# Half-height transposes in two row tiles, and a filter spectrum stored with both runs of a partition together

## The chip, the cores and the metric

The kernel runs on one core of a Trainium2 chip. The metric is the device time of one execution in microseconds, as the median of several runs. A profiled execution is one further run; its span goes from its first to its last instruction.

## What is computed

A gated recurrence over 6272 steps, followed by a gated long convolution, for 4 batches of 256 channels:

```python
sig = 1.0 / (1.0 + np.exp(-f_logit))
f = lower_bound + (1.0 - lower_bound) * sig
i = 1.0 - f
for t in range(S):                       # S = 6272
    h = f[:, t] * h + i[:, t] * x[:, t]
    y[:, t] = h
...
proj = y @ w_proj                        # 256 -> 3 * 256: x1, x2, x3
X2 = np.fft.rfft(x2, n=S, axis=1)
H = np.fft.rfft(filter_fft, n=S, axis=0)
x2_conv = np.fft.irfft(X2 * H, n=S, axis=1)
out = (x1 * x2_conv * x3) @ w_out
```

The inputs and the output are float32, x and f_logit are 4 x 6272 x 256.

## The kernel before

The Fourier transforms are written as matrix products. 6272 is 49 x 128, so a transform is done as one over 128 points and one over 49, each with a small table of cosines and sines as one operand on TensorE. Channels are worked in 16 units of 8 pairs.

**Opening.** `prepare` builds the tables, loads the filter (L576), rotates it with matmuls (L587), transforms it (`first`, L612, and `second`, L630), and writes the spectrum of each unit to device memory (`hst`, L638), because it doesn't fit beside the rest. TensorE is kept running with warm-up matmuls (`warm`, L557); four of the 32 warm-up groups (L555) are made of eight half-height transposes each. At the same time `hgrn(0)` computes the recurrence of the first batch.

**Recurrence.** `hgrn(b)` goes through 13 chunks of 512 time steps (the last has 128). A chunk of x and f_logit is loaded with time along the partitions, four steps to each (L302, into XT and FL, three buffers each). ScalarE takes the sigmoid in place (`sig`, L304), GpSimd multiplies it onto x (`u`, L306). For each half of the channels (kh) TensorE turns both so that channels lie along the partitions and time along the row: `sT` for the sigmoid and `uT` for the product, each of four transposes of 128 x 128 into one PSUM bank (L313). A transpose takes one of the four columns of a partition and so writes every fourth element of the bank. `f` makes the gate from the bank of sT (L327 on ScalarE, L329 on VectorE), and `scan` runs the recurrence on VectorE over the bank of uT (L335) into HA, which holds the whole sequence of a batch, with a wrapped copy of its front part (`wrap`).

**Spectrum.** `phase_p` projects the columns (P, L670) and evacuates them into X2 (`x2`). For each unit, F1 (L683) and its evacuation `A` do the first step, F2 (L728) the second, two `prod` on VectorE (L741) multiply by the spectrum in Hu, I2 (L751) starts the inverse and `Th` evacuates. `mini`, `zm` and `slot` do a few special frequencies. Hu has three buffers; `H` (L718) fills one per unit and batch. In device memory a unit's spectrum is a matrix of 98 + 64 rows of 2 KB: rows 0 to 97 are the spectrum, and rows 98 to 161 repeat its first 64. Partition p needs rows p and p + 49, and `twice` (L265) describes that read.

**Gates and output.** `gate` computes x1 and x3 (x13, L362), evacuates them (`xs`) and multiplies them on GpSimd (`z`, L378). `phase_o` ends the inverse (I1, L784), multiplies on VectorE (`y`, L790), projects (L802), evacuates (`o`) and stores (L812).

F2, mini, I1, FF2 (`second`) and `last` work with matmuls of 64 rows, two at a time in the upper and the lower half of the array, which write to two neighbouring PSUM banks. All other TensorE work uses the full height, or 98 rows of it.

**What sets the order.** Each step is recorded by `Plan.op` with its kind, its cost on each engine that may do it, what it reads and writes, and how many PSUM banks it takes (`take`). Nothing is scheduled when the kernel is built: `ORDER` (L117) is a table made beforehand, three letters for each step, which give the step, the engine and the first PSUM bank. `Plan.emit` goes through it once. So each engine has its own fixed sequence, DMAs are all issued by SyncE (SP) in the table's order, and a step starts when it is at the head of its engine and its semaphores allow it.

In time, the work of a batch stands so that P is followed by a stage of units (F1, F2, prod, I2, and x13 of the gates) and one of output (I1, y, proj). The recurrence of the next batch is laid into the unit and output stages of the one before; there is none after the last transposes at 392.8 us.

Of the kernel before, what the change touches and what calls it, by code (L numbers as in the profile page):

```python
# [10 lines left out]
F32R = mybir.dt.float32r  # L11
# [10 lines left out]
S = 6272  # L22
D = 256
# [35 lines left out]
class Plan:  # L59

    ROWS = ("F2", "mini", "I1", "FF2", "last")
# [56 lines left out]
    "BLgAAYA8gAOYABIAsQBBgACIBGgA0RBagBVgAbSBQgBkgAfUA7YAPIAtVADgAdWBfgA9YAwQERgA+RBCAApTAqUBABBpgAoVBHABDWARIAuQ"  # L118
    "BugBMYBEGAgTBFGA6UA/BBITBzgBNVBJDA2QBKDB4gAjXBRYBPFAkRAQAAlSESgBWYA5QEfgBSTAnXBTLBbYBXRBOFEggAmQBUDBZJAYYBcV"
    "BgAAUIA3XBYJEtgAvQASABlIBhTBeFAeREugBjDA4XBqIBiDBmQETAAcSAFgBoIBvYAzXBnIAxUBrSBdNBwQB0YAWIBtCAiXBsKB5AArUATI"  # L120
    "ByAAEYB6VB1SB8NBxAEUYB7NAhXB3KB2CEVUCBVEXMEhAB/QCKSEWXCLCEaUEiYEYPCCFCISE7gCAACTVCJCEcMCEQCNSCFICDYEbXAVYCUF"
    "CMYEjUEvAE8gEdPEkWCcQEwYEoVElMCdAEpXFJgCOCEmOCaQCHgExUFKgCbACRSCQgEzMEqFEyWCSCClQE0OE9ACVYCWUCeYCfSCmAErPE+Y"
    "E2WCXEE3QCgKE/RE4GCZgCjUFXgFBBCsWFYgE5IAZYCkECGgFASFLAFETFCKC1UFlgCtGCnYCoQFMYCPgAHAFGLCuWCpIFFSCvGFNTC2EC3W"
    "FHKAaYFPDFOQFZAFSRFQIFTUFxgC4GFbVCwYCigAIADHSFmgC5YFUJFaYAJAFygC6WFdFFVMCrgCxQCYgC7GAyVChgDIKC+UB9YCyIDJWC/E"
    "DASDKGFcUFnADBKFgVFeMDDQDCYF9gALADLYAXYFzACqgDMWDEIDQSFiFFoYFhUDRCDSQFjMF+gDbSDTAFpVAMADZQAKAFrNF0YFqUDaAFtV"
    "FsMDNGFuQGJgF1RGKgDVWDcKF3BDUYF2UFvNDdYDWGFRYDkSFwIFWYF5RF/ADeVGVgF4MF7BF6XC0gDlCGAYDtQGWgDfFDiSDuIGBUDjKDrV"
    "GLAGDMD0QEeYGCSDsFF8PDmYGFTGMYDnUGhgGEKGHDGGWD1AGNXGigGIOD2SGPHCzgDvYGOQGXAGRRD3KD9WGtgGQIGTBDwSGYYC9gFkAC8g"
    "GSRD+GGZQE6AGUJGugD/WGbADGgDFgE1YGjAGaQEAOD4YDXgGdRGcIEBYGeWGkYAGgGfBGlXDOgDoEGgOD5QDYgFIAEGUDPgDxKGnHMwgFfY"
    "GmWEHEEsYGpXGvAGoOEIUGrHGwYGqSEJEGxTGyXGsKA1WD6AEKYFDYG1UEPVANAGzLECQEQFG0PEZYELSEnYJsXG3EG5gMvgEMCB+YG2VJtW"
    "DpgG4NM9gJxUJvGG8SEOgEDAHGVG9KEEgD8gHAQHHFDqgJzMENgJySNLgHBIJuHHKTJ0CJwYDygMxAHCVHLLHOQMyYHDFEFgHESDzgHPAM+g"  # L130
    "G6UHFCJ1YJ2XHSQJ4HHMSHTIM/AHQWG7EHIQHROHNCG+UHJAHegJ3WG/MMzXHlgJ5GJ7SD7gNNAJ6YJ8TM1PDggHUQDhgJ9KJ+DNMgHWUHVI"
    "KAWJ/YHXEKBXHYSKDHHfQNAYHZCHmUHiIKFXKCGHaSKHHHhIKGWKEYM0RKIGM4XHoMHbCHzgKKQKJYKLWHsgKMAHcSM2JKPUKNGKQQM6HKOY"
    "KUWHdKKSAM5RHpMKRENBXHgYKWGH8SKTYNDHNCQM7JIEgH6UH9CNZgHnYKVWKZXH7EKXONGRNEIHjSKYYKbHNIBHtUM8AH0WHwMKaQHkCKeR"
    "KcAHvMHqSKgBKdYKfVHrCH3OH+QILgKjUM3YNagH/AIASH1YKlMHuYKkXNOYKhFH2OHxQIBCIFUHyIISgKmHICSNHWNngNbAIDKIgQKiYKoX"
    "IHMIhAKpSKnYKtTKrCNJOH4QKqHKuUH5AKsYIIMKySKzXKwEIMQKvDIGYK1PIZgIiUK0CKxYNogIOIK3WIjENPTINYNQXIPIK2YNRDK4SK5G"
    "IJUNSPK6CIqgNcYITQIKEIkSIWINpANUWNVXN1gNWGIVINdUIUYN2gNqYIlCIQVNXPIxgIaQNfEImSIRFIcIK8UInCIbYIXVK7YIdIK9XIYF"
    "LBQIoSK/HIrVI4gIpKLDALCRItNK+ENeXN3ALGSLAYLHTNgPIeULEBIsYLICLFYJGQIuNLJDNiXIfENjSODgIzYNkPNrTNTYJHAI/gJIULKY"
    "NlKIyWNtDIvQJJEN4YI1OLLTLMSLNDI0OI5UIwANsXLOCNYYI7MLQTJQgJKQLPYOEgLSDLRWI8MJLANwSI6YLVUOPgNyCI2QNuPJXgJASI3A"
    "LTOLWVJMQJDKLUYLYFLaXJNANxWJCKN5VNvYOQgLXEJOQLbTN7FLZYJPIJegN6ULcHNzOLfSNhAN+VJBYNmYLhCI9QObgN8MOAFJRWLdDLgS"
    "I+AJUOLeYLkVJETOFAJTOJSYJYQJZYLmFOGYN/XJFDJbIJlgOHVLiCOcgJVTOJFJaIJfRJWDLjYLlWJiJORAJcTLpVLnGJhJLqQLoYOISLsA"  # L140
    "OLWLrFOBPJmQJgYJdDJnYOSYSJVJoIJjTONGSLFOMXJpIJkDSKWOogOTQLtYOngSMGSOVOKKOdAJqTOUROOPOeYOVAOXWOYSJrDOzgOfQOWJ"
    "O0gOZGLuTSQFLzWLvLOhASPROgVSRBL0OOjQOpALwTO/gOaKL4WOqYLxDOkRL5OOlAOrSPAgL1TO1ALygOmJNFYL6WL2DO2YOiNL9QL7GL3g"
    "MCTL+IOsVN0AOvWNKYOCAMDLOwXOtCN9YPLgL/QL8gOxGOuNPMgMESMAAOyPO3UMBgMHVO5EMMQMINMFCO4XO7UPBAMNIMJSVMgPNAMGgPCY"
    "O9EO8VO6PPDWMKCMOQO+NMLgMRSMPAPOYMWUMSKPFGMbQPEXVOAMXMPHWMTSPJGVagPGPMQgMYUQJgMUCMcIPIWMZEPPXPQSPTTPKOMdQVog"
    "PRHVNgPUUPSKVQVMVgPVDMgWVbgPWMVSFP7gMlSMhOMagPrUMeAMmKPjWPsEPlQPkGPnSPZUPoCPfWPaMVqAPbSPmAPgOPdUPcCPhQPeEPXW"
    "PiAPpSPYOVcAPvUPtQPwMPqCMiWPuAMqSMnUMjGMrKSNYMkgPxQMoEQCgPzSPyIVPYP3WP0CP1UP4OSTQP2EP8RSVASSYQDWP+JP5TSUVSYQ"
    "P6LSWFSZRSaAP/JP9YQXTSXYSbBSdVQYDQZQQGOQQgSeSQEYMfgScYQaAQATQFOSiXSfFQLYSjQSgCQBLQhgQKVSlAShYQHRSkHQMNSnQSmY"
    "QIBSoTQNNQRUSqDQSYQiRSpAQTMQogQOWSrYVpgSsTQUMQPGStQVdYSxUQkJQVWQvgSzESuDQbUQWGQlJSyTVRRQcEQdWSvIVVSS0DVTJSwY"
    "VWUQeGV2gS2VQ2gS3QVXCS1YV3gQpWS4FQfRS7TQgJS5AVeVS9DQrOQqYQ/QS6YVgFVfSRAAVjTVYMS8VQjYWEgTAWS+FVhKQ9QTCGS/YTBU"
    "VlDMsVQsOQ+ATFSTDETGTMtNTHKQwQV4AMugTEYTILRHgQmVTKXVrYQnFQzIQtSTMHRBUQyIQuCQ3WRCETLRTJYQ6OROgRDSVkQRECTPUQ4Y"  # L150
    "Q5OQxYVsVTNBQ0STREVmITOYRVgRIWVuFWFgTQRQ1CRKOQ7UTSBRjSRLOQ8ETTYRFQRkCRWURGIRcgRPWWGATUSRJYRSORQYV5YRlQTWCTVT"
# [722 lines left out]
```

## Time and profile before

| | us |
|---|---|
| median of 3 runs | 485.76 (485.37 to 486.49) |
| profiled execution | 484.15 |
| its span | 482.3 |
| transposes (L313), 784, busy | 121.5 |
| prod (L741), 128, busy | 147.1 |
| scan (L335), 104, busy | 122.8 |
| f on ScalarE (L327), one of 512 | 0.700 |
| first P group of the four batches starts at | 79.4, 182.2, 289.2, 394.0 |

"Busy" of an engine is the time in which at least one of its instructions ran; instructions overlap with the next one, so that the mean duration of one, times their number, is more than they occupy. What they occupy when the engine is full is the distance from one start to the next. The memory traffic is 116.39 MB, 64 reads of the spectrum with 392 KB each, and 16 writes each of 196 and of 128 KB. The granted clock of TensorE is 0.997 on average.

### The profile page before, as it was taken

What the parts mean: (1) busy time and instruction counts of PE and PEld (TensorE: products, weight loads), DVE (VectorE), ACT (ScalarE), POOL (GpSimd) and SP (SyncE); (2) the same over time, 40 slices, a digit from 0 to 9 for tenths busy, and PEclk for the clock granted to TensorE, in tenths of its full rate; (3) what the DMA queues carried; (4) which work ended last, traced back from release to release, by engine and by line L of the source; (5) the groups of instructions that cost most, each with busy time, mean ns of one, the idle gap of its engine ahead of it and who ended that gap; (6) DMA issues with size and microseconds to landing.
All of it is one profiled execution on the core that took longest, in us unless ns stands there. A gap on an engine that the chain in (4) does not pass through costs nothing.

```text
span 482.3 us, 13258 instructions
## 1 busy us (share of the span) xinstructions
PE 467.0 (97%) x5273; PEld 374.9 (78%) x5273; DVE 425.5 (88%) x456; ACT 416.5 (86%) x609; POOL 298.4 (62%) x307
## 2 busy tenths in 40 slices
PE   8999999999999999999999999999999999999995
PEld 6887877877778999776778889667788998676694
DVE  8879997699999995899999998999999975999983
ACT  5979989999999888989989785999989978999664
POOL 6769775679778620787789533677698332755700
PEclk9999999999999999999999999999999999999998
DMA  8989989847685989476668989364778864345266
GB/s 331 377 277 297 330 283 279 283 153 238 197 296 176 305 293 310 130 250 211 207 211 270 349 280 331 114 195 157 265 264 307 319 228 154 102 132 153 66 262 274
DMA packets 41725, 116.39 MB, mean 241 GB/s; under 512 B 4384, under 2 KB 6304, under 8 KB 41664
## 3 DMA queue, kind: packets, MB, share of 16 engines
q1 hardware_dynamic: 41664, 115.56, 71.5%
q8 instruction: 41, 0.67, 0.6%
q14 instruction: 20, 0.16, 0.1%
HBM read 84.54 MB, written 31.00 MB: 240 GB/s over the span
## 4 chain that ended last, share of the span: by engine, by line
PE 70%; DMA 9%; DVE 7%; ACT 6%; issue 3%; POOL 2%; SPq 0%; POOLq 0%; DVEq 0%; ACTq 0%
PE PS L313 14%; PE PS L362 14%; PE PS L751 8%; PE PS L670 7%; PE PS L802 7%; PE PS L728 6%; PE PS L683 5%; DMA X<-in_moe_filter_fft_dram 4%; DMA out_dram<-osb 4%; PE PS L612 3%; PE PS L784 3%; DVE PP L741 2%; DVE HA L335 2%; ACT osb L275 2%; PE PS L630 2%
## 5 line engine op out<-in xcount | busy, mean ns | idle before, releaser
L378 POOL TENSOR_TENSOR zt<-x1s,x3s 128x490 f16<-128x490 f32 (+1 forms) x104 | 125.8, 1217 | 85.0 <-DVE ys L790 27.5
L741 DVE TENSOR_TENSOR PP<-PS,Hu 98x1008 f16<-98x1008 f32 x128 | 147.1, 1198 | 4.4 <-PE PS L728 1.4
L306 POOL TENSOR_TENSOR XT<-XT,FL 128x1024 f32<-128x1024 f32 (+1 forms) x52 | 116.9, 2251 | 47.0 <-ACT FL L304 28.9
L335 DVE TENSOR_TENSOR_SCAN HA<-fTs,HA,PS 128x512 f16<-128x512 f32 (+1 forms) x96 | 113.0, 1203 | 4.4 <-PE PS L313 1.6
L362 PE MATMUL PS<-HA,W 128*128 128x490 f16 (+1 forms) x416 | 107.2, 368 | 0.0
L327 ACT ACTIVATE fTs<-PS,nomc 128x512 f32<-128x512 f32 (+1 forms) x90 | 60.5, 674 | 7.5 <-PE PS L313 3.9
L275 ACT ACTIVATE osb<-PS 128x1024 f32<-128x1024 f32 (+1 forms) x51 | 49.9, 992 | 17.8 <-PE PS L802 12.0
L790 DVE TENSOR_TENSOR ys<-PS,zt 128x1024 fp32r<-128x1024 f32 (+1 forms) x52 | 59.0, 1153 | 6.9 <-PE PS L784 2.2
L313 PE MATMUL PS<-iden,XT 128*128 128x128 f32 x392 | 61.2, 276 | 0.9 <-ACT fTs L327 0.4
L273 ACT CAST HA<-PS 128x1024 f16<-128x1024 f32 x57 | 57.9, 1027 | 2.8 <-PE PS L683 2.1
L313 PE MATMUL PS<-iden,FL 128*128 128x128 f32 x392 | 60.3, 274 | 0.0
L751 PEld LDWEIGHTS <-PP 98*128 98x128 f16 x1024 | 50.0, 98 | 11.2 <-issue 3.5
L273 ACT COPY x3s<-PS 128x490 f32<-128x490 f32 (+1 forms) x93 | 53.5, 577 | 4.6 <-PE PS L362 2.9
L275 ACT ACTIVATE x1s<-PS 128x490 f32<-128x490 f32 (+1 forms) x93 | 53.9, 591 | 3.7 <-PE PS L362 2.0
L802 PE MATMUL PS<-Wo,ys 128*128 128x256 f32 x392 | 56.4, 291 | 0.6 <-DVE ys L790 0.2
L304 ACT ACTIVATE FL<-FL 128x1024 f32<-128x1024 f32 (+1 forms) x52 | 53.1, 1024 | 1.7 <-DMA FL<-in_f_logit_dram 1.7
L362 PEld LDWEIGHTS <-W 128*128 128x128 f16 x416 | 34.6, 98 | 23.3 <-issue 6.4
L751 PE MATMUL PS<-VA,PP 98*128 98x98 f16 x512 | 52.0, 207 | 0.7 <-POOL PP L733 0.3
L313 PEld LDWEIGHTS PS<-iden,XT 128*128 128x128 f32 x392 | 44.7, 140 | 9.5 <-issue 3.0
L273 ACT CAST Th<-PS 128x784 f16<-128x784 f32 x58 | 47.8, 826 | 4.9 <-PE PS L751 4.0
L802 PEld LDWEIGHTS PS<-Wo,ys 128*128 128x128 f32 x392 | 49.2, 188 | 3.5 <-DVE ys L790 1.2
L751 PE MATMUL PS<-VB,PP 98*128 98x98 f16 x512 | 51.7, 207 | 0.0
(114 smaller groups left out, 695.9 us busy)
## 6 DMA issues: line engine op xcount, KB each, us to landing
Hu<-H SPq DMA_DIRECT2D x64, 392.0 KB
FL<-in_f_logit_dram SPq DMA_DIRECT2D x48, 512.0 KB
XT<-in_x_dram SPq DMA_DIRECT2D x48, 512.0 KB
out_dram<-osb SPq DMA_DIRECT2D x48, 512.0 KB
X<-in_moe_filter_fft_dram SPq DMA_DIRECT2D x9, 512.0 KB
H<-Hu SPq DMA_DIRECT2D x16, 196.0 KB
H<-Hu SPq DMA_DIRECT2D x16, 128.0 KB
Hu<-in_moe_filter_fft_dram SPq DMA_DIRECT2D x2, 512.0 KB
```

Of the source, the lines that this page charges most:

```text
L273: nc.scalar.copy(dst, src)
L275: nc.scalar.activation(dst, src, AF.Copy, scale=scale)
L306: op("u", {"POOL": 0.1 + 0.553 * nb}, lambda e, xt=xt, ft=ft: nc.gpsimd.tensor_tensor(xt, xt, ft, op=AOP.mult), r=[("ft", k)], w=[("xt", k)])
L313: nc.tensor.transpose(PS[:, p, j:128 * nb:nb], src[:, j, cols], iden[:])
L327: nc.scalar.activation(fT, PS[:, p, 0:n], AF.Identity, scale=by, bias=1.0)
L335: nc.vector.tensor_tensor_scan(h, fT, PS[:, p, 0:n], init, op0=AOP.mult, op1=AOP.add),
L362: nc.tensor.matmul(PS[:, p, 0:n], W13[:, kh, js], HA[:, HB[kh] + t0:HB[kh] + t0 + n], start=(kh == 0), stop=(kh == 1))
L378: nc.gpsimd.tensor_tensor(late["zt"][:, jb, :, m0:m0 + nm], xs(0), xs(1), op=AOP.mult),
L741: nc.vector.tensor_tensor(PP[:TB, k, o, :, :, 1:64], px.unsqueeze(1).broadcast_to([TB, 2, UE, 63]), hh[:, :, :, 1:64], op=AOP.mult)
L751: nc.tensor.matmul(PS[:, ib + o, pr * TB:(pr + 1) * TB], PP[:TB, k, o, n, 2 * pr:2 * pr + 2, :], v[:TB], start=(n == 0), stop=(n == 1))
L790: nc.vector.tensor_tensor(late["ys"][:, yk, :, 0:rn * 128], PS[:, cb:cb + 2, 0:rn * 128], late["zt"][:].rearrange("p k r m -> p k (r m)") ...
L802: nc.tensor.matmul(po[:, i, :], late["ys"][:, yk, kh, i * 128:(i + 1) * 128], Wo[:, kh, :], start=(kh == 0), stop=(kh == 1))
```

## The change

There are three parts.

1. `sT` and `uT` become one step `su`. Each transpose of 128 rows becomes two of 64 rows, in the upper and the lower row tile, and 16 of these make a `su` (four in the last chunk). The upper half writes into the first of two neighbouring banks, the lower half into the second. The sigmoid lies in the outer quarters of the two banks (elements 0 to 255 and 768 to 1023), the product in the middle (256 to 767). So `f` reads two runs, and `scan` one run that crosses from one bank into the other. `su` reads both the sigmoid and the product, and takes two banks.
2. The spectrum of a unit is kept in memory as 98 x 2 rows of 2 KB, so that the two rows that a partition needs lie side by side and are read as one run of 4 KB. It is written with three transfers (98, 49 and 49 rows) in place of two (98 and 64).
3. `ORDER` is a new table, with 2350 steps in place of 2438. The four warm-up groups of half-height transposes become warm-up matmuls like the others.

```diff
-    ROWS = ("F2", "mini", "I1", "FF2", "last")
+    ROWS = ("su", "F2", "mini", "I1", "FF2", "last")
...
-    H = [dram.tile([TB + 64, 2 * UE * 64], F16, name=f"H{u}") for u in range(NU)]
+    H = [dram.tile([TB, 2, 2 * UE * 64], F16, name=f"H{u}") for u in range(NU)]
...
+    def bank(pb):
+        return PS[:, pb:pb + 2].rearrange("p a t -> p (a t)")
+    def halves(pb, hn):
+        a = PS[:, pb, 0:hn]
+        return bass.AP(tensor=a.tensor, offset=a.offset,
+                       ap=[a.ap[0], [768, 2], a.ap[1]])
...
-                def turn(e, p, src, cols=cols, nb=nb):
-                    for j in range(nb):
-                        nc.tensor.transpose(PS[:, p, j:128 * nb:nb], src[:, j, cols], iden[:])
-                sT = op("sT", {"PE": 0.109 * nb}, lambda e, p, f=turn, s=ft: f(e, p, s),
-                        r=[("ft", k), "iden"], w=["qT"], take=1)
-                uT = op("uT", {"PE": 0.109 * nb}, lambda e, p, f=turn, s=xt: f(e, p, s),
-                        r=[("xt", k), "iden"], w=["qT"], take=1)
+                hn = 64 * nb
+                def turn(e, pb, ft=ft, xt=xt, cols=cols, nb=nb, hn=hn):
+                    for src, at in ((ft, (0, 768)), (xt, (512 - hn, 512))):
+                        for j in range(nb):
+                            for p in range(2):
+                                ps = slice(64 * p, 64 * p + 64)
+                                nc.tensor.transpose(bank(pb)[:, at[p] + j:at[p] + hn:nb],
+                                                    src[ps, j, cols], iden[ps, ps])
+                su = op("su", {"PE": 0.126 * nb}, turn, r=[("ft", k), ("xt", k), "iden"], w=["qT"], take=2)
...
-                        nc.scalar.activation(fT, PS[:, p, 0:n], AF.Identity, scale=by, bias=1.0)
+                        nc.scalar.activation(fT, sT, AF.Identity, scale=by, bias=1.0)
...
-                   nc.vector.tensor_tensor_scan(h, fT, PS[:, p, 0:n], init, op0=AOP.mult,
+                   nc.vector.tensor_tensor_scan(h, fT, bank(pb)[:, 512 - hn:512 + hn], init, op0=AOP.mult,
...
-            for i, (p0, n) in enumerate(((0, TB), (TB, 64))):
-                op("hst", {"SP": 0.36}, lambda e, hw=hw, u=u, p0=p0, n=n: nc.sync.dma_start(
-                    H[u][p0:p0 + n], hw[0:n].rearrange("p e k -> p (e k)")),
+            for i, (a, d, p0, n) in enumerate(((0, 0, 0, TB), (1, 0, Q, Q), (1, Q, 0, Q))):
+                op("hst", {"SP": 0.36}, lambda e, hw=hw, u=u, a=a, d=d, p0=p0, n=n: nc.sync.dma_start(
+                    H[u][d:d + n, a, :], hw[p0:p0 + n].rearrange("p e k -> p (e k)")),
...
-            Hu[:TB, h].rearrange("p a e k -> p a (e k)"), twice(H[u][:])),
+            Hu[:TB, h].rearrange("p a e k -> p a (e k)"), H[u][:]),
```

## The prediction

> **What bounds the kernel now.** I read the page first: the engines' busy shares (part 1), the slices (part 2), then the groups with their shapes kept apart, the timeline of TensorE around the instructions that the change replaces, and last a table of busy time by stage.
>
> ```profile
> PE 467.0 (97%) x5273; PEld 374.9 (78%) x5273; DVE 425.5 (88%) x456; ACT 416.5 (86%) x609; POOL 298.4 (62%) x307
> ...
> PE   8999999999999999999999999999999999999995
> ...
> DVE  8879997699999995899999998999999975999983
> ACT  5979989999999888989989785999989978999664
> ...
> PEclk9999999999999999999999999999999999999998
> ```
>
> PE is the longest engine, 467.0 of 482.3 us, at full granted clock. But DVE and ACT stand close behind, and the slices show where they leave room: at the start, in four dips and at the end. So an average says little; I cut the trace at the first and last projection group of each batch (L670) and the first inverse group (L784). Columns: stretch, length, busy us of PE, PEld, DVE, ACT, POOL, clock, DMA share, GB/s.
>
> ```profile
> 0.00:79.40 79.40, 75.84 (x595) 61.35 (x596) 68.44 (x103) 66.20 (x100) 59.37 (x79) 1.00 0.90 314
> ...
> 182.20:193.10 10.90, 10.82 (x101) 10.67 (x98) 5.75 (x6) 9.73 (x11) 0.00 (x0) 1.00 0.89 314
> 193.10:259.50 66.40, 65.64 (x763) 48.37 (x763) 62.74 (x65) 60.64 (x95) 52.80 (x52) 1.00 0.68 213
> 259.50:289.20 29.70, 28.84 (x377) 26.39 (x377) 28.40 (x27) 25.23 (x35) 15.14 (x11) 1.00 0.88 296
> ...
> 456.20:474.70 18.50, 18.37 (x282) 16.53 (x284) 14.35 (x12) 10.18 (x10) 0.79 (x1) 1.00 0.64 254
> ```
>
> The reader is to see three kinds of stage. In a P stage (182.2 to 193.1) only PE is full, and no transpose runs in it. In the unit and output stages (193.1 to 289.2) PE is full, DVE at 94 to 96%, ACT at 85 to 91%: take work from PE and DVE is next, 1 to 4 us later. The last batch has no transposes at all (the last one starts at 392.8), so from 394 on nothing is taken away.
>
> **The change, part by part.** Transposes first. These are the old ones, and below them three of four warm-up groups of the kernel before that have the new form (the fourth is of another type):
>
> ```profile
> L313 PE MATMUL PS<-iden,XT 128*128 128x128 f32 x392 | 61.2, 276 | 0.9 <-ACT fTs L327 0.4 <-ACT osb L275 0.3
> L313 PE MATMUL PS<-iden,FL 128*128 128x128 f32 x392 | 60.3, 274 | 0.0
> ...
> L555 PE MATMUL PS<-iden 64*128 64x64 f32 x24 | 1.7, 266 | 0.0
> ```
>
> The mean of one (276 ns) is its latency; what counts is the distance between starts. From the timeline of PE:
>
> ```profile
> 5.23 0.27 PE L557 MATMUL PS<-iden 128*128 128x256 f16 x1
> 5.43 0.47 PE L555 MATMUL PS<-iden 64*128 64x64 f32 x8
> 5.83 0.61 PE L557 MATMUL PS<-iden 128*128 128x256 f16 x4
> ```
>
> ```profile
> 100.44 0.60 PE L313 MATMUL PS<-iden,XT 128*128 128x128 f32 x4
> 100.88 0.60 PE L313 MATMUL PS<-iden,FL 128*128 128x128 f32 x4
> 101.32 0.61 PE L683 MATMUL PS<-D,X 128*128 128x128 f16 x8
> ...
> 104.57 0.21 PE L751 MATMUL PS<-VB,PP 98*128 98x98 f16 x1
> 104.71 1.05 PE L728 MATMUL PS<-HA,FT 64*128 64x256 f16 x16
> ```
>
> Four full transposes take 0.44 us, 0.1093 each by their single starts; 784 of them are 85.7 us of PE. In the L555 line the single records start two at a time, 5.422, 5.543, 5.605 and 5.667, and the next instruction at 5.824: a pair of halves costs 0.0625, the first pair 0.0575 more. Changing between full height and row tiles costs about 0.095 each way: from the last L751 to L728 are 0.14 us where L751's own distance is 0.043, and L557, 0.109 apart by itself, is 0.20 from L555.
>
> After the change one `su` (four columns, two sources) is 8 pairs: 0.0575 + 8 x 0.0625 = 0.558, against 0.875 for sT and uT. There are 96 of these and 8 of a quarter size (2 pairs, 0.183): 55.0 us. The two orders say how often PE changes between full and half height: 190 times before (198 with the warm-up halves), 244 after, so 46 x 0.095 = 4.4 us. PE in all: -85.7 + 55.0 + 4.4 = -26.3 us.
>
> A rule speaks against this. The Trainium skill, TensorEngine Tiling (Array Packing), section Performance Considerations, says that each matmul carries some 60 cycles of overhead, so that tiling should not be had by shrinking a dimension that is already small; here the moving side shrinks from 128 to 64 columns and 1568 instructions replace 784. An estimate from that page: L557 streams 256 columns in 0.109 us, 0.43 ns each, so 60 cycles are 26 ns on top of 55 (half of a full transpose's distance), 0.081 a pair, 0.71 a su, and the sum for PE would be -11.8. The row has 0.0625, overhead included; I take the row.
>
> What no row shows: outputs of half height with a step. L555 wrote its 64 columns side by side, su writes every fourth element. The same skill, PSUM — Partial Sum Buffer, section Specifications (TRN2), warns that output which isn't contiguous slows matmuls significantly. The nearest row is L313 itself, which writes every fourth element and takes 0.1093 for 128 columns, 0.85 ns a column against 0.98 in L555: no loss from the step at that rate, and each row tile has a bank of its own. Bounds: 0.0545 a pair (half a full one) to 0.109 (halves one after the other), with which PE's sum would be +10.4 in place of -26.3. I take 0.0625, the row of the same instruction.
>
> Evacuation: f reads two runs of 256 out of two banks in place of 512, scan the same 512 across a bank border. xs reads PSUM in steps of 49 at 0.465 us for 490, 0.95 ns an element beside 0.88 for the copies of A, so I put 0 on it (0 to 0.05 each; below zero is excluded, the elements are as many; at most 5 us on either engine). Counts per engine move little in the new order: by distances between starts (prod 1.115, scan 1.187, y 1.131; ACT: A 0.904, f 0.582, xs 0.465, Th 0.705) DVE has 413 us before and 411 after, ACT 391 and 391.
>
> Memory: the filter spectrum is read in 98 packets of 4 KB in place of 196 of 2 KB. A packet takes 159 ns against 84 in the trace, so 64 reads save 64 x (16464 - 15582) ns / 16 = 3.5 us of DMA share, which nothing on the path waits for (share 0.63 to 0.68 in the unit stages). It is written with three transfers, 196 packets in place of 162: 16 x 34 x 84 ns / 16 = 2.9 us more in the opening, plus 16 more issues on SP, behind which the loads of x and f queue. There DMA is at 0.90 of 79.4 us, 71.5. In this part it counts.
>
> A su waits for sigmoid and for u where sT waited for the sigmoid alone, and it holds both banks until scan has ended. Behind it on PE's queue is everything else. The order puts it late enough in the plan; its price is a rival below.
>
> The sum goes by stage. I counted what each order puts between the marks and multiplied by these distances; the largest engine of a stage is its floor. Before: opening PE 72.4 (measured 79.4); P stages PE 10.8 to 11.6 (10.9 to 12.3); unit stages 63.2, 62.8, 61.0, 46.8 (66.3, 66.4, 62.2, 50.8); output stages 24.4, 28.3, 29.4, 17.9 (25.0, 29.7, 30.3, 18.5); end 1.5 (7.6). Floors sum to 453.3, measured is 482.3, and what is left over is 29.0, of it 7.0 in the opening and 6.1 at the end. After: opening PE 64.7; P 10.8, 11.8, 10.8, 10.8; units 61.1 (ACT, PE only 58.8), 59.1 (PE), 61.3 (DVE), 48.6 (PE); outputs 24.2, 28.1, 28.0 (all DVE), 17.7; end 1.5: 438.5. So 14.8 less in place of 26.3: the rest goes into time in which PE stands and DVE or ACT is full. If the same 29.0 is left over, the opening would be 71.7; but its DMA has 71.5 + 2.0 (the 34 of 48 spectrum writes that stand in it) - 1.3 (one load fewer) = 72.2, which at the 0.97 that the best stretch (12 to 24 us) shows is 74.4. I take the middle, 73.5, 1.8 over. -14.8 + 1.8 = -13.0 from the profiled execution's 484.15 (span 482.3, 1.85 around it). The median shown is 485.76, 1.6 above: 472.8.
>
> **The rivals.** All of PE's 26.3 us is on the path, since the order was laid anew around a shorter PE: 459.5. For it: PE is 97% busy. Against: DVE and ACT have 123 us free between them, and at a span of 456 they would have 70, of which the opening, the P stages and the end already hold most.
>
> Two banks held: su keeps two from first transpose to the scan's end, 0.56 + 0.70 + 1.27 = 2.5 us each, 5.1 bank-us, against 1.14 + 1.71 = 2.85 before, 215 bank-us over 96 su or 6% of eight banks. If PE waits 0.1 us at each of 104 su, 10 us of the gain go: about 482. For it: PE's full slices leave few banks idle. Against: before all 784 old transposes PE stood idle for 0.9 us.
>
> The slower side: the stepped halves don't overlap. At 0.109 a pair su is 0.93 against 0.875; 91.7 us against 85.7, plus 4.4 of changes, all on PE's path: +10.4, 496. It decides from 0.095 a pair on, where PE gains nothing. This is also the case in which the change doesn't do what it says.
>
> **How the numbers follow.** DVE and ACT take over: 0.58, 464 to 479, likeliest 472.8. All on the path: 0.11, 455 to 464. Banks: 0.14, 480 to 488, half of it below the measurable. No overlap: 0.17, 489 to 505. A measurement of this kernel tells 0.2% (1 us) from no change. Faster 0.58 + 0.11 + 0.07 = 0.76, same 0.03, slower 0.04 + 0.17 = 0.21. The range leaves out most of both ends: 461 to 489.
>
> **What would show it.** In the profile after: starts of su pairs 0.0625 apart and su 0.56 long; PE's busy sum 20 to 26 us lower and its share under 96% while DVE rises above 89%; the first P group at 72 to 75; the last batch (first P to end) still 88 to 90 us. I am wrong if pairs are 0.1 apart, if PE shows many waits before su, if f or scan is longer than 0.70 and 1.27, or if the opening stays at 79 with DMA at 0.95.

## The result and the profile after

| | before | after |
|---|---|---|
| median of 20 runs each, us | 485.88 (481.99 to 490.36) | 489.03 (484.55 to 494.24) |
| ratio, with its 95% interval | | 1.0054 [1.0030, 1.0077] |

The change makes the kernel slower by 0.54%; the forecast was 472.8 us. A second set of runs of the changed kernel gave 487.32 against 485.70, ratio 1.0036 [1.0014, 1.0058]. The profile taken with the first set fell in a disturbed execution (494.24 us at a lower clock), so the profile after is the one of the second set: 486.83 us, span 485.0.

Its page, parts 1, 2 and 4 (PE had 97% and nearly nothing but 9 before):

```profile
PE 446.6 (92%) x6041; PEld 343.6 (71%) x6041; DVE 427.0 (88%) x456; ACT 417.1 (86%) x607; POOL 298.0 (61%) x309
...
PE   8888999999989889999898889998999889999995
...
DMA  8989987765598997254768989198568960466267
...
PE 30%; DMA 13%; DVE 7%; ACT 4%; issue 3%; SPq 0%; POOL 0%; ACTq 0%; DVEq 0%
```

The last two kinds of line, from the page of the kernel before:

```profile
DMA  8989989847685989476668989364778864345266
...
PE 70%; DMA 9%; DVE 7%; ACT 6%; issue 3%; POOL 2%; SPq 0%; POOLq 0%; DVEq 0%; ACTq 0%
```

TensorE did give up what it was to give up: 467.0 to 446.6 us of busy time, in a span that is 2.7 us longer. VectorE and ScalarE didn't take its place; their totals are the same as before and their shares too (88 and 86%). Nothing is full. The lines of the chain that ended last aren't to be compared as they stand: their shares are of the whole span, and after the change the chain can be followed back only to 201.4 us, so that they add up to 57% (before: 97%). In the part that both have, summed from the pieces of the chain, TensorE holds 69% before (from 200 us on) and 52% after, and transfers 6% (18 us) and 22% (62 us). In the DMA row there is now a slice of 1 between two of 9, and further on one of 0: before, the lowest was 2, in the last stretch of the kernel, and 3 ahead of it.

By stage, with the same marks as in the prediction (columns again: stretch, length, busy us of PE, PEld, DVE, ACT, POOL, clock, DMA share, GB/s):

```profile
0.00:78.20 78.20, 68.59 (x773) 54.27 (x774) 70.00 (x103) 67.85 (x99) 59.39 (x80) 1.00 0.90 329
...
154.50:182.20 27.70, 23.39 (x432) 20.57 (x432) 25.72 (x25) 22.40 (x32) 15.24 (x14) 1.00 0.98 345
...
193.90:258.30 64.40, 61.72 (x841) 42.25 (x841) 57.61 (x60) 58.99 (x93) 46.51 (x47) 1.00 0.55 178
258.30:290.20 31.90, 27.37 (x486) 23.18 (x482) 29.62 (x27) 27.57 (x39) 20.58 (x17) 1.00 0.88 318
290.20:302.20 12.00, 10.94 (x101) 10.64 (x98) 6.01 (x6) 9.80 (x11) 2.37 (x1) 1.00 0.97 353
...
366.10:397.40 31.30, 28.31 (x489) 24.20 (x488) 29.34 (x28) 26.53 (x38) 15.75 (x11) 1.00 0.91 320
397.40:408.00 10.60, 10.60 (x102) 10.52 (x97) 7.95 (x8) 6.71 (x7) 2.44 (x2) 1.00 0.01 2
```

and the first and the third output stage of the kernel before (the second stands in the prediction):

```profile
157.10:182.10 25.00, 24.87 (x344) 22.74 (x342) 24.17 (x23) 21.67 (x30) 10.42 (x8) 1.00 0.91 294
...
363.70:394.00 30.30, 29.75 (x383) 26.75 (x383) 29.49 (x27) 25.94 (x37) 15.04 (x11) 1.00 0.85 308
```

The first three output stages (from 154.5, 258.3 and 366.1) became longer, 25.0, 29.7 and 30.3 before and 27.7, 31.9 and 31.3 after (DMA share 0.98, 0.88 and 0.91), although TensorE has less to do in them. Length times GB/s is what a stage moves: the first output stage 25.0 x 294 = 7.4 MB before and 27.7 x 345 = 9.6 MB after, the second unit stage 66.4 x 213 = 14.1 and 64.4 x 178 = 11.5. The other two output stages grow from 8.8 and 9.3 to 10.1 and 10.0 MB. So the new table moves transfers into the output stages, out of the second unit stage and out of P stages: at 397.4 us, in the last of these, the memory is idle. The first output stage is full of transfers (share 0.98): at 353 GB/s, the best rate of any stretch above, its 9.6 MB take 27.1 of its 27.7 us. In the other two the share is 0.88 and 0.91, and what the transfers cost there has to be read from the waits. The loads follow the recurrence. Counted as full transposes (two halves for one), the output stages hold 70, 91 and 85 before, and 84, 104 and 100 after; the unit stages 132, 104 and 108 before, and 112, 95 and 96 after. An output stage also has the stores of its batch.

Who waits for transfers is seen in the waits (engine, tile and line; what it waited for; us in total, times, longest). First after, then before; the line numbers differ by a few between the two:

```profile
ACT FL L307 <- DMA FL<-in_f_logit_dram: 9.1, 9, 1.6
ACT osb L268 <- DMA out_dram<-osb: 7.1, 10, 1.4
POOL XT L309 <- DMA XT<-in_x_dram: 7.0, 6, 2.8
DVE PP L740 <- DMA Hu<-H: 6.3, 6, 1.6
...
DVE osb L273 <- DMA out_dram<-osb: 2.6, 1, 2.6
```

```profile
POOL XT L306 <- DMA XT<-in_x_dram: 9.5, 4, 7.3
...
ACT osb L275 <- DMA out_dram<-osb: 4.4, 6, 1.4
...
ACT FL L304 <- DMA FL<-in_f_logit_dram: 1.7, 3, 1.1
```

ScalarE, VectorE and GpSimd waited 15.6 us for these transfers before and 32.1 after. ScalarE, which evacuates many of the banks, has half of that (9.1 and 7.1), and what it does late, TensorE gets late: see the next view, the groups of TensorE after. Behind the bar stand busy time and mean ns, then the idle time before the group and its releasers:

```profile
L321 PE MATMUL PS<-iden,FL 64*128 64x64 f32 x784 | 44.8, 230 | 7.9 <-ACT osb L268 4.2 <-DVE HA L342 1.6 <-DVE PP L740 0.7
L321 PE MATMUL PS<-iden,XT 64*128 64x64 f32 x784 | 42.0, 223 | 1.9 <-POOL XT L309 1.9
```

Before all transposes TensorE now stands 9.8 us, where it stood 0.9. The releaser named first is the evacuation of an output tile (osb), in nine waits. The longest of them is this one:

```profile
161.51 0.46 PE L321 MATMUL PS<-iden,FL 64*128 64x64 f32 x8 [1.23 <-ACT osb L268]
```

and this is what ScalarE did before it:

```profile
159.49 1.06 ACT L307 ACTIVATE FL<-FL 128x1024 f32<-128x1024 f32 x1 [1.21 <-DMA FL<-in_f_logit_dram]
160.45 1.92 ACT L268 ACTIVATE osb<-PS 128x1024 f32<-128x1024 f32 x2
```

ScalarE had stood 1.21 us for a load of f_logit, and the evacuation behind it came late. The second longest (0.83 us, at 383.8) follows an evacuation that had itself waited 1.29 us for a store. So late loads and late stores both reach TensorE through ScalarE.

### The profile page after: what moved, and what is told of

Read it like the earlier page. It is cut to its first block, busy times and chain, and to the rows that moved or that the text cites. A ratio compares the mean times of both kernels' runs of the same rounds, so it can differ in the third digit from the quotient of the medians.

```text
span 492.5 us, 14714 instructions
## 1 busy us (share of the span) xinstructions
PE 449.5 (91%) x6041; PEld 346.5 (70%) x6041; DVE 426.1 (87%) x456; ACT 417.8 (85%) x607; POOL 298.2 (61%) x309
## 4 chain that ended last, share of the span: by engine, by line
PE 30%; DMA 11%; DVE 8%; ACT 4%; issue 3%; POOL 0%; SPq 0%; ACTq 0%; DVEq 0%; POOLq 0%
PE PS L369 9%; PE PS L750 5%; DMA out_dram<-osb 4%; PE PS L727 4%; DVE PP L740 3%; PE PS L669 3%; DMA FL<-in_f_logit_dram 3%; PE PS L682 3%; DVE HA L342 3%; DMA Hu<-H 2%; PE PS L321 2%; PE PS L801 2%; ACT osb L268 2%; DMA XT<-in_x_dram 1%; DVE ys L789 1%
## 5 line engine op out<-in xcount | busy, mean ns | idle before, releaser
L369 PE MATMUL PS<-HA,W 128*128 128x490 f16 (+1 forms) x416 | 106.0, 369 | 4.2 <-DVE PP L740 1.7
L307 ACT ACTIVATE FL<-FL 128x1024 f32<-128x1024 f32 (+1 forms) x52 | 52.9, 1021 | 11.6 <-DMA FL<-in_f_logit_dram 11.5
L334 ACT ACTIVATE fTs<-PS,nomc 128x512 f32<-128x512 f32 (+1 forms) x89 | 59.4, 684 | 3.0 <-PE PS L321 2.3
L268 ACT ACTIVATE osb<-PS 128x1024 f32<-128x1024 f32 (+1 forms) x46 | 45.8, 1015 | 18.9 <-PE PS L801 9.7
L801 PE MATMUL PS<-Wo,ys 128*128 128x256 f32 x392 | 57.5, 294 | 2.2 <-ACT osb L268 1.4
L268 ACT ACTIVATE x1s<-PS 128x490 f32<-128x490 f32 (+1 forms) x95 | 56.2, 597 | 3.8 <-PE PS L369 2.9
L266 ACT CAST Th<-PS 128x784 f16<-128x784 f32 x60 | 49.8, 834 | 5.2 <-PE PS L750 5.0
L750 PE MATMUL PS<-VB,PP 98*128 98x98 f16 x512 | 52.9, 208 | 0.0
L321 PE MATMUL PS<-iden,FL 64*128 64x64 f32 x784 | 44.7, 230 | 7.4 <-ACT osb L268 2.9
L321 PEld LDWEIGHTS PS<-iden,FL 64*128 64x128 f32 x784 | 33.6, 138 | 22.2 <-DVE HA L342 5.3
L669 PE MATMUL PS<-W,HA 128*128 128x256 f16 x392 | 45.2, 276 | 1.7 <-ACT X L266 1.7
```

The source lines that it names most:

```text
L266: nc.scalar.copy(dst, src)
L268: nc.scalar.activation(dst, src, AF.Copy, scale=scale)
L321: nc.tensor.transpose(bank(pb)[:, at[p] + j:at[p] + hn:nb], src[ps, j, cols], iden[ps, ps])
L369: nc.tensor.matmul(PS[:, p, 0:n], W13[:, kh, js], HA[:, HB[kh] + t0:HB[kh] + t0 + n], start=(kh == 0), stop=(kh == 1))
L669: nc.tensor.matmul(pp[:, r - r0, :], column(HB[kh], q_of(r)), W2[:, kh, :], start=(kh == 0), stop=(kh == 1))
L750: nc.tensor.matmul(PS[:, ib + o, pr * TB:(pr + 1) * TB], PP[:TB, k, o, n, 2 * pr:2 * pr + 2, :], v[:TB], start=(n == 0), stop=(n == 1))
```

## The experiments

The theory after this comparison: the new table asks for more transfers in the output stages than they can take, and the time won on TensorE is spent waiting for them. The rivals: half-height transposes cost more in the kernel than their distances say; the new layout of the spectrum costs time; a `su` that holds two banks makes TensorE wait; the queue of SyncE has the transfers in a bad order.

In the kernels with halved loads, stores or sigmoids and in those without the scan, part of the work is left out or replaced, as the expectations say. Their time shows what the left-out part costs; none is a kernel that could be used. "Before" in the same group of runs was 485.5 to 487.6, and each kernel is compared with it; a difference between kernels of different groups carries up to 2 us of that spread. Openings and stages are read from one profiled execution each.

### The parts of the change, one at a time

The changed kernel again:

> The changed kernel as it is, on the same chip as the three others. Its profile on record had an opening of 79.2 us, first P groups at 79.2, 187.9, 296.3 and 404.8 and a span of 492.5. Expected 488 to 490 us (ratio 1.003 to 1.008), PE busy 445 to 452, the loads of f_logit and x waited for by ScalarE and GpSimd for 20 us and more, and stretches of 8 us and more in which no load is on its way because SyncE's queue stands before a read of the spectrum.

Measured 487.32, ratio 1.0036 [1.0014, 1.0058], just under the range. TensorE's busy time was as expected (446.6); ScalarE and GpSimd waited 16.1 us for f_logit and x, not 20 and more.

The old layout in the changed kernel:

```diff
-    H = [dram.tile([TB, 2, 2 * UE * 64], F16, name=f"H{u}") for u in range(NU)]
+    H = [dram.tile([TB + 64, 2 * UE * 64], F16, name=f"H{u}") for u in range(NU)]
...
-            for i, (a, d, p0, n) in enumerate(((0, 0, 0, TB), (1, 0, Q, Q), (1, Q, 0, Q))):
+            for i, (p0, n) in enumerate(((0, TB), (TB, 64), (0, 0))):
...
-            Hu[:TB, h].rearrange("p a e k -> p a (e k)"), H[u][:]),
+            Hu[:TB, h].rearrange("p a e k -> p a (e k)"), twice(H[u][:])),
```

> The changed kernel with the old layout of the spectrum in memory (two writes of 98 and 64 rows, read as two runs of 2 KB); order and transposes stay new. If the layout costs (2.9 us more of writes in the opening): 2 to 3 us faster than the changed kernel, all of it before the first P group. If the layout is paid by nothing on the path: equal within 1 us. If the 4 KB packets were a gain: up to 2 us slower.

Measured 489.09, ratio 1.0072 [1.0041, 1.0102]. That is 1.8 us above the changed kernel, with intervals that overlap: in the new table the layout costs nothing that can be seen.

The new layout in the kernel before (the second and third write are issued one right behind the other):

```diff
-            for i, (p0, n) in enumerate(((0, TB), (TB, 64))):
+            for i, parts in enumerate((((0, 0, 0, TB),), ((1, 0, Q, Q), (1, Q, 0, Q)))):
```

> The kernel before with the new layout of the spectrum alone (third write issued right behind the second). If the layout costs in the opening: 1 to 3 us slower than before. If it does nothing: within 1 us. If 4 KB packets are a gain: 1 to 3 us faster.

Measured 489.17, ratio 1.0076 [1.0047, 1.0104]: 3.5 us more. So the new layout has a price in the old table and none that can be seen in the new one. Where it lies isn't shown: the opening is 80.9 in place of 79.4 us, but it is 81.7 in a kernel below that leaves the opening as it was (half stores), and the first unit stage is 67.5 in place of 66.3.

Full-height transposes in the changed kernel, in the same `su` and the same table:

```diff
-                    for src, at in ((ft, (0, 768)), (xt, (512 - hn, 512))):
+                    for src, p in ((ft, pb), (xt, pb + 1)):
                         for j in range(nb):
-                            for p in range(2):
-                                ps = slice(64 * p, 64 * p + 64)
-                                nc.tensor.transpose(bank(pb)[:, at[p] + j:at[p] + hn:nb],
-                                                    src[ps, j, cols], iden[ps, ps])
+                            nc.tensor.transpose(PS[:, p, j:128 * nb:nb], src[:, j, cols], iden[:])
```

> The changed kernel with full-height transposes inside su (8 of 128 x 128, source by source, in the same two banks); order and layout stay new. Theory A (PE is no longer the bound of the new order, VectorE, ScalarE and transfers are): PE gets some 26 us more work, most of it falls into time in which PE stands, and the kernel is 3 to 10 us slower than the changed one. Theory B (PE is still the bound): 20 to 26 us slower, 509 to 515. Theory C (the half-height transposes are themselves what costs, by their two banks or their switches): equal or faster.

Measured 496.04, ratio 1.0193 [1.0156, 1.0230]. That is 8.7 us slower than the changed kernel, as Theory A had it (3 to 10). Two things follow. The half-height transposes are worth 496.0 - 487.3 = 8.7 us in this table. And the new table with the old transposes is 10.3 us slower than the old table with them (485.7). That gap also holds the layout and the two-bank `su`.

### The transfers

Half of each load of x and f_logit (after the first three chunks), in the changed kernel, in the one before, and in the changed one with full-height transposes:

```diff
-                    dst, src[b, t0:t0 + n, :].rearrange("(p j) d -> p j d", p=128)),
+                    dst[:, 0:nj], src[b, t0:t0 + n, :].rearrange("(p j) d -> p j d", p=128)[:, 0:nj]),
```

> The changed kernel, but from the fourth chunk on each load of f_logit and x brings in only two of the four rows of a partition (256 KB for 512; the rest is left from before, so values are not the reference's; all instructions of the engines are the same). 24 MB of 117 MB are left out. Theory A (in the new order the opening and the output stages stand on transfers): opening 72 to 75 in place of 78.2, output stages 25 to 30 in place of 27.7, 31.9, 31.3; in all 472 to 478, 10 to 15 us under the changed kernel. Rival (the new order is long because of its waits between engines, transfers only come last by chance): 483 to 487, at most 4 us less.

> The kernel before with the same halved loads (same piece of the computation spoiled). Theory A (the old order is bound by TensorE, transfers matter little): 481 to 485, 1 to 5 us less than before. Rival (transfers limit the old order just as much): 472 to 477.

> Halved loads and full-height transposes in the new order (the difference to the kernel with halved loads alone is the worth of the half height when transfers are light; 8.7 us with full loads). Theory A: transfers hid a part of the saving, so the difference grows, to 10 to 18 us: 485 to 492. Rival (VectorE and ScalarE hid it): difference unchanged, 6 to 10 us.

Half of each store, in the changed kernel and in the one before, and loads and stores halved together:

```diff
-                out[b].rearrange("(a r) d -> a r d", r=Q)[:, r0:r0 + rn, :],
-                late["osb"][k][:, 0:rn, :]),
+                out[b].rearrange("(a r) d -> a r d", r=Q)[:, r0:r0 + (rn + 1) // 2, :],
+                late["osb"][k][:, 0:(rn + 1) // 2, :]),
```

> The changed kernel with only two of four rows of each output group stored (half of the output is left unwritten; instructions of the engines as before). Theory A: the opening stays at 78, the three output stages that hold loads and stores come down by 2 to 4 us each: 476 to 481. Rival (waits between engines): 484 to 487.

> The kernel before with half stores (every store writes the first half of its rows). Half loads gave it 1.8 us. If stores bind only the new table, 483.5 to 486; if the output stages are bound by stores in both tables, 477 to 481 as in the changed kernel.

> The changed kernel with half loads of x and f_logit (chunks after the first three of batch 0) and half stores at once, so that half of the input stays stale and half of the output isn't written. Alone they gave 476.8 and 478.6 against 487.3. If transfers and engines overlap so that one relief is enough, both together give 474 to 477 (what is left is engines waiting for each other). If the two add up, 466 to 470, and transfers alone hid the whole of the 14.8 us forecast.

Medians in us, with the ratio to the kernel before of the same group where it wasn't given above:

| | old table, full height | new table, full height | new table, half height |
|---|---|---|---|
| all transfers | 485.5 to 487.6 | 496.0 | 487.3 |
| half loads | 483.7, 0.9960 [0.9934, 0.9985] | 486.9, 1.0028 [1.0006, 1.0050] | 476.8, 0.9838 [0.9786, 0.9891] |
| half stores | 483.7, 0.9934 [0.9904, 0.9964] | | 478.6, 0.9877 [0.9817, 0.9936] |
| both | | | 474.1, 0.9749 [0.9701, 0.9797] |

In the old table a relief of the transfers is worth 1.8 (485.5 - 483.7) and 2.7 us (486.3 - 483.7). In the new one it is worth 10.5 and 8.7, and 13.2 together: the two don't add up, since each relieves the same stages. With half loads the half-height transposes are worth 10.1 us (486.9 - 476.8); against the 8.7 without, that is no difference that these runs could tell, so whether the transfers hid a part of their saving isn't decided. But half loads are worth 9.1 us in the new table with full-height transposes too (496.0 - 486.9), and the new table's handicap shrinks from 10.3 to 3.2 us (486.9 against 483.7). So it is the table that has the transfer problem, not the transposes. Half loads and half stores gave the times that Theory A had for them, but with half loads the opening stayed at 77.7 us, where Theory A had 72 to 75.

The first output stage of the kernel with both halved:

```profile
153.30:177.90 24.60, 23.36 (x433) 20.59 (x433) 24.46 (x24) 21.94 (x31) 15.23 (x14) 1.00 0.66 211
```

and the first group of transposes with both halved, with half loads alone and with half stores alone:

```profile
L321 PE MATMUL PS<-iden,FL 64*128 64x64 f32 x784 | 44.7, 230 | 4.3 <-DVE HA L342 1.9 <-DVE PP L740 0.7 <-issue 0.5
```

```profile
L321 PE MATMUL PS<-iden,FL 64*128 64x64 f32 x784 | 45.0, 231 | 4.0 <-DVE HA L342 1.7 <-DVE PP L740 0.7 <-ACT fTs L334 0.5
```

```profile
L321 PE MATMUL PS<-iden,FL 64*128 64x64 f32 x784 | 44.9, 230 | 5.7 <-ACT osb L268 1.8 <-DVE HA L342 1.7 <-DVE PP L740 0.8
```

The instructions are the same as in the changed kernel. The first output stage falls from 27.7 to 24.6 us, with VectorE full in it (24.46), which is what the prediction expected of all three; the other two take 29.9 and 30.0. That is hardly shorter than before the change (25.0, 29.7 and 30.3), since VectorE was nearly full there already (24.17, 28.40 and 29.49). The wait of TensorE for osb is gone with both halved and with half loads alone (4.2 to at most 0.5 us), and 1.8 is left with half stores alone. So what looked like a shortage of banks here was late transfers, loads even more than stores. The 1.9 us of waits for the scan that are left are what can be put down to the two banks of a `su`. The opening doesn't move (77.9), though its DMA share fell from 0.90 to 0.76.

### The queue of SyncE

Loads and spectrum reads go through one queue, in the table's order. The timeline of that queue at the start of the second unit stage (start, length, what was issued), after and before:

```profile
202.15 0.33 SPq L717 DMA_DIRECT2D Hu<-H  x1
...
204.38 26.43 SPq L717 DMA_DIRECT2D Hu<-H  x10
...
231.32 0.38 SPq L304 DMA_DIRECT2D XT<-in_x_dram  x1
```

```profile
207.44 0.40 SPq L301 DMA_DIRECT2D XT<-in_x_dram  x1
209.31 0.31 SPq L718 DMA_DIRECT2D Hu<-H  x1
212.44 0.36 SPq L301 DMA_DIRECT2D FL<-in_f_logit_dram  x1
```

After, ten spectrum reads stand in a row over 26 us, and no load is issued between 182 and 231; before, loads stand between the reads. Did the reads block the loads? A load needs a free buffer, and a buffer is free when both `su` of its chunk are done. This is the work of the transposes from 182.2 us, where the P stage ahead begins, to the next `su` (stretch, length, busy us of PE and PEld for L321 alone, clock, DMA share, GB/s), and then the two next `su` in TensorE's timeline (the lines of FL):

```profile
182.20:222.90 40.70, 0.00 (x0) 0.00 (x0) 1.00 0.48 162
```

```profile
223.01 0.46 PE L321 MATMUL PS<-iden,FL 64*128 64x64 f32 x8
...
230.36 0.46 PE L321 MATMUL PS<-iden,FL 64*128 64x64 f32 x8
```

Three sigmoids had run by 193 us, so all three buffers were full; for 41 us the table has no transposes, and the first buffer came free with the second `su`, near 231 us. The load at 231.32 follows at once. So in this stretch it is the place of the transposes in the table that holds the loads back, and not the reads ahead of them in the queue.

The experiment put the question to the whole queue. In the changed kernel all transfers of the queue were sorted by the moment at which their buffer or their data was ready in its profile; then the same in the kernel before; then in the changed one with stores and spectrum writes left at their old times. Only letters of `ORDER` change places.

> The changed kernel with one thing moved: the transfers in SyncE's queue are sorted by the time at which, in the profile of the changed kernel, the last instruction that each waits for had ended (buffer free, or data ready). No other engine's order changes, and no transfer is added or left out. In that profile a transfer stands 4.7 us on average between being ready and being issued, and 89 of 285 stand over 3 us. Theory A, the order of SyncE's queue is what makes the transfers late (loads behind spectrum reads that wait for a buffer): 477 to 483 us, and the waits of ScalarE for f_logit and of VectorE for the spectrum fall from 9.1 and 6.3 us to under 5 in all. Theory B, the transfers are too many for the stages in which the new table needs them, whatever their order in the queue: within 2.5 us of 487.3.

> The same sorting of SyncE's queue in the kernel before, by its own profile (4.5 us on average from ready to issue, 74 of 269 over 3 us). Theory A puts the blame on the new table's queue, so here there is little to gain: 484 to 487. If both kernels gain alike, by 4 us or more, the queue costs time in any order and doesn't explain the difference between the two. Theory B: within 2.5 us of 485.7 also.

> As the first kernel, but stores and spectrum writes keep the times at which they were issued before; only loads and spectrum reads go by readiness. If stores that come earlier take bandwidth from the loads, this one is 2 us or more faster than the one in which all are sorted; Theory A has it at 477 to 483, Theory B within 2.5 us of 487.3.

Measured 508.79 (1.0464 [1.0413, 1.0515]), 513.08 (1.0567 [1.0517, 1.0618]) and 507.28 (1.0430 [1.0363, 1.0497]). None of the expectations has this. The loss of the first lies in the opening:

```profile
0.00:98.30 98.30, 72.23 (x773) 57.12 (x774) 68.45 (x103) 68.25 (x99) 59.59 (x80) 0.90 0.79 286
```

```profile
POOL afs L273 <- DMA X<-in_moe_filter_fft_dram: 10.9, 2, 10.7
```

Loads whose buffers are free at the start went ahead of the last three parts of the filter, which GpSimd waits for here and TensorE after it, and 20 us went. The other two lose in the opening as well (93.4 in place of 79.4 us and 93.9 in place of 78.2). Behind the opening the first needs 408.2 us where the changed kernel needs 485.0 - 78.2 = 406.8, the second 417.6 where the one before needs 402.9, the third 413.1. The output stages of the first are 27.4, 31.8 and 34.1 us against 27.7, 31.9 and 31.3 (the 34.1 at a granted clock of 0.95), and its waits of ScalarE for f_logit rose to 14.3 us in place of falling. The row of spectrum reads is still there, with the first load behind it at 249.98:

```profile
221.93 27.32 SPq L714 DMA_DIRECT2D Hu<-H  x11
```

By readiness too, then, no load belongs between these reads, which agrees with the buffers above. So this order gains nothing in the stages in question, and in the stretch looked at it is the table that places what needs the transfers too densely. For the other stretches a better order of the queue isn't excluded.

### The opening

TensorE has 7 us less to do in the opening (75.8 to 68.6), and it got 1.2 us shorter. Even that is within the scatter of single profiles: half stores leave the opening alone, and in the two kernels with them it is 79.3 (changed) and 81.7 us (before), where 78.2 and 79.4 stand above. From 30 us on ScalarE is busy 46.0 of 48.2 us and VectorE 45.1. Each was relieved alone: half of the sigmoid of batch 0, then a multiply in place of its scan, each also in the kernel before, and then both together with half loads.

```diff
-            op("sig", {"ACT": 0.095 + 0.213 * nb}, lambda e, ft=ft: nc.scalar.activation(
-                ft, ft, AF.Sigmoid, scale=-1.0), w=[("ft", k)], table="sigmoid")
+            op("sig", {"ACT": 0.095 + 0.213 * nb}, lambda e, g=ft[:, :, 0:128] if b == 0 else ft: nc.scalar.activation(
+                g, g, AF.Sigmoid, scale=-1.0), w=[("ft", k)], table="sigmoid")
...
-                   nc.vector.tensor_tensor_scan(h, fT, bank(pb)[:, 512 - hn:512 + hn], init, op0=AOP.mult,
-                                                op1=AOP.add),
+                   nc.vector.tensor_tensor(h, fT, bank(pb)[:, 512 - hn:512 + hn], op=AOP.mult) if b == 0 else
+                   nc.vector.tensor_tensor_scan(h, fT, bank(pb)[:, 512 - hn:512 + hn], init, op0=AOP.mult, op1=AOP.add),
```

> The changed kernel; in batch 0 alone the sigmoid is taken for half of the channels (the other half keeps the logit, so the output differs). It takes some 5 us from ScalarE in the opening (12.25 full sigmoids of 0.95 us, half of each) and nothing from any later stage, from TensorE, VectorE or the transfers. Theory E: the opening of the changed kernel is set by ScalarE, which from 30 us on is busy 46.0 of 48.2 us (VectorE 45.1): opening 74 to 76 in place of 78.2, kernel 483 to 485 against 487.3. Theory T, the opening waits for transfers (DMA share 0.90), or for banks that a su holds: opening stays within 0.7 of 78.2.

> The kernel before with the same half sigmoid in batch 0. Theory E: here TensorE is busy 30.0 of 30 us from 30 to 60 us and sets the pace as well, so less is won: opening 78 to 79.4, kernel 484.5 to 486. Theory T: no change.

> The changed kernel with the recurrence of batch 0 left out: in that batch VectorE multiplies the gate by the bank with one tensor_tensor in place of the scan, with the same inputs and output (so the output differs). It takes some 12 to 15 us from VectorE in the opening (25 scans of 1.2 us; a multiply of the same size is put at 0.6, half of y's 1.13 for 1024 elements) and frees the two banks of a su sooner. Theory V: the opening is set by VectorE, busy 45.1 of 48.2 us from 30 us on: opening 71 to 75 in place of 78.2, and the kernel shorter by as much, 480 to 484. Theory T, transfers set it (DMA share 0.89): opening 77 or more.

> The kernel before with the same edit. From 30 us on TensorE is busy 48.8 of 49.4 us there, so Theory V has little to gain: 77 to 79.4. If this opening falls as much as that of the changed kernel (to 75 or less), VectorE's scans held both and TensorE, though full, didn't set the pace.

> The changed kernel with the three reliefs of its opening at once: half loads of x and f_logit, half of the sigmoid of batch 0, and a multiply in place of the scan of batch 0 (so the output differs). One at a time they left the opening at 77.7, 77.6 and 80.0 us. Theory J, several resources bind it jointly (when one is relieved the next takes over): opening 70 to 73, kernel 467 to 471. Theory L, it is held by a chain that goes from engine to engine, with TensorE's own order in it, which no relief of VectorE, ScalarE or the loads shortens much: 76 or more, kernel 473 to 477 by the loads alone.

| | median, us | ratio | opening, us |
|---|---|---|---|
| changed kernel | 487.32 | 1.0036 | 78.2 |
| half sigmoid | 488.82 | 1.0044 [1.0013, 1.0075] | 77.6 |
| no scan | 487.37 | 1.0022 [0.9982, 1.0061] | 80.0 |
| half loads | 476.79 | 0.9838 | 77.7 |
| all three | 473.32 | 0.9734 [0.9667, 0.9801] | 75.4 |
| before, half sigmoid | 485.45 | 0.9990 [0.9953, 1.0027] | 80.7 |
| before, no scan | 484.98 | 0.9986 [0.9946, 1.0026] | 83.2 |

The opening after 30 us with all three reliefs:

```profile
30.00:75.40 45.40, 41.63 (x576) 33.71 (x573) 32.54 (x47) 41.66 (x70) 38.19 (x45) 1.00 0.70 220
```

Four us of ScalarE (46.0 to 41.7) and 12 of VectorE (45.1 to 32.5) were taken away, and with the loads halved as well the opening gives 2.8 us. One at a time the reliefs left it at 77.6 to 80.0 us, no change beyond the scatter, where Theories E and V had 71 to 76; in the kernel before it became no shorter either (80.7 and 83.2). So none of the three sets it alone. The last expectation had 70 to 73 for a joint bound and 76 or more for a chain through the engines; 75.4 is in neither and nearer to the second. That the fixed orders of the engines, TensorE's among them, hold the opening in a chain is argued from this and not shown; the cause stays open.

## Why the prediction was wrong

The step that failed is "If the same 29.0 is left over". The work of the engines fell about as reckoned (TensorE's in the opening by 7.2 us of busy time, where the floors had 7.7), but what was left over the floors was not the old 29.0: the span is 485.0, and 485.0 - 438.5 = 46.5. The old rest belonged to the old table. By carrying it over, the prediction left the waits for transfers outside the opening as they were in the old table, without looking at where the new table puts the transfers. By kinds of stage, with the forecast (the prediction's floors, and for each kind what was left over before), the changed kernel and the one with loads and stores halved:

| us | forecast | after | after, transfers halved |
|---|---|---|---|
| opening | 73.5 | 78.2 | 77.9 |
| four P stages | 44.7 | 45.0 | 43.6 |
| four unit stages | 242.0 | 244.2 | 241.8 |
| four output stages | 101.5 | 110.3 | 102.9 |
| end | 7.6 | 7.3 | 6.1 |
| span | 469.3 | 485.0 | 472.3 |

With loads and stores halved, unit and output stages come within 1.4 us of the forecast, which speaks for the counts, the distances and "VectorE is next". Of the 15.7 us that were missing, halving takes away 12.7. Not all of that is new with the table: in the old one half loads are worth 1.8 and half stores 2.7 us (both together were not run). The rest is the opening, partly made up by the P stages and the end.

Point by point:

- **Price of a pair.** Right. Within the eight transposes of one source, pairs start 0.062 apart (median; 85% between 0.061 and 0.065), with outputs that step by four. The timeline of TensorE in the first output stage:

```profile
155.04 0.41 PE L321 MATMUL PS<-iden,FL 64*128 64x64 f32 x8
155.29 0.41 PE L321 MATMUL PS<-iden,XT 64*128 64x64 f32 x8
155.54 0.61 PE L783 MATMUL PS<-ID,Th 64*128 64x128 f16 x16
155.99 0.42 PE L321 MATMUL PS<-iden,FL 64*128 64x64 f32 x8
...
156.63 2.34 PE L801 MATMUL PS<-Wo,ys 128*128 128x256 f32 x16
```

  From 155.04 to 155.54 a whole `su` takes 0.50; the extra 0.0575 of the first pair doesn't appear between two steps in row tiles. From row tiles into the full height (155.99 to 156.63) it is 0.64, so this change costs 0.14, where the prediction had 0.095 for a change and 0.0575 for the first pair. Neither the overhead that the Trainium skill states for each matmul (TensorEngine Tiling (Array Packing), Performance Considerations; it would have made 0.081) nor its warning of strided outputs (PSUM — Partial Sum Buffer, Specifications (TRN2)) shows here. The rival in which halves don't overlap is out; that its sign was right is luck.
- **TensorE's sum.** -26.3 forecast, -20.4 by busy time, inside the 20 to 26 that were named.
- **Evacuation.** Right: `f` takes 0.700 before and after, `scan` 1.270 and 1.269, and VectorE and ScalarE total 427.0 and 417.1 us where they had 425.5 and 416.5.
- **Layout.** Forecast at 2.0 us of transfer time in the opening. Taking the layout back made the changed kernel no faster (489.1 against 487.3). A price is seen in the old table alone (3.5 us).
- **Transfers.** This is the term that was left out: they were costed in the opening and nowhere else. The prediction took the counts of each engine's work from the new table, but not where the loads fell, though the table sets it: 12, 15 and 8 loads are issued in the first three output stages against 9, 11 and 7 before. The row it showed itself (259.50, DMA at 0.88 and 296 GB/s, against a best of some 350) had room for a sixth more, and more was to be moved in a stage that was to become shorter.
- **Opening.** Forecast 73.5 by transfers (the middle of its 71.7 and 74.4 is in fact 73.05), 78.2 measured, and halved loads leave it at 77.7: the bound named was not the bound. Nor is ScalarE or VectorE alone. Open.
- **Two banks held.** This rival said 0.1 us at each `su`, 10 us in all (472.8 and 10 are 483, not the 482 it gave). The view agrees (9.8 us of idle time before the transposes), but by luck for most of it: with the transfers relieved 5.5 are left (4.3 above, and 1.2 before the second group, which waits for GpSimd), and 1.9 of these are waits for the scan to free banks.
- **What would show it.** The tests of the pair, of the busy sum, of TensorE's share (92%) and of `f` and `scan` were met while the time went the other way. The first P group at 72 to 75 was not (78.2), and the last batch took 87.6 us, just under its 88 to 90. VectorE over 89% was not met: it is at 88% after as before, while TensorE's share fell. No engine had become the next bound, and this line tells that the gain went into waiting.

No kernel here that does the whole computation is faster than the one before.

## What to carry to other kernels

An edit that comes with a new order has two effects, and the floor of each stage must be made for every resource of the new order, transfers included: MB in the stage divided by the best rate that the trace shows for a whole stage. What was left over under the old order isn't a constant that may be carried on to the new one. When a full engine gets faster and no other engine's share rises, look at who waits for transfers, and halve loads or stores in an otherwise equal kernel to see what that waiting costs.

## What the runs showed of the hardware

Two half-height fp32 transposes in the two row tiles mostly (91%) start within 10 ns of each other, and a pair takes 0.062 us where one of full height takes 0.109. So the halves run at the same time, and a pair is some 14% dearer than half of a full one (0.0545).

In the kernel with the sorted queue TensorE stood idle for all of 22 to 27 us; the clock granted in that stretch is 0.50, and 0.56 in the 9 us after it (columns as above):

```profile
22.00:27.00 5.00, 0.00 (x0) 0.00 (x0) 0.00 (x0) 0.00 (x0) 0.00 (x0) 0.50 1.04 405
27.00:36.00 9.00, 5.47 (x27) 4.48 (x28) 2.62 (x5) 2.83 (x5) 5.62 (x9) 0.56 0.23 91
```

So this idle stretch cost more than itself. An estimate: at 0.56 of the clock the 5.47 us of work that follow are worth some 3 (5.47 x 0.56) at full speed. It is one case, and which length of idle time lowers the clock was not measured.
